# Conversion order of two networks' weights, and the turn of the global rows, in a fused attention and FFN kernel

## The chip, the cores and the metric

The kernel runs on one core of a Trainium2 chip. The metric is the device time of one execution in microseconds, from runs on the chip.

## The reference

Four batches of 8 heads attend locally (512 tokens, a window of 32 to each side, plus 32 global tokens); the 32 global rows of each batch attend to everything. The 2304 x 512 result goes through two feed-forward networks, the first gated, the second with a rational function in place of the gate:

```
x = attention(q_l, k_l, v_l, q_g, k_g, v_g)     # 2304 x 512
gate = 1 / (1 + exp(-(x @ w_gate)))
x = (gate * (x @ w_val)) @ w_out                # 512 -> 1536 -> 512
h = x @ w2_in                                   # 512 -> 2048
P = a0 + a1*h + a2*h*h + a3*h*h*h
Q = 1 + |b0|*|h| + |b1|*h*h
out = (P / (Q + 1e-6)) @ w2_out                 # 2048 -> 512
```

The inputs come as 64-bit numbers; the kernel turns their two 32-bit words into single precision itself.

## The kernel before

**Products.** Every product of the two networks is made of three matmuls on a high and a low part: line 710 to 712 for a first product (rows times inner weights), 828 to 830 for the second product of the gated network, 1240 to 1242 for that of the rational one. A weight therefore exists as a pair of halves, hi and lo.

**Conversion.** An item of weights comes as a raw DMA of 512 KB, and is then worked on by four engines: `magnitude` (two instructions on ScalarE, lines 564 and 565), `bits` (two on DVE, 572 and 573), `add` (one on POOL, 580), `hi` (a cast on ScalarE, 602) and `lo` (a subtraction on POOL, 610); most parts are then kept in DRAM and loaded again when they are wanted. For the gate and value weights `sums` (DVE, 627 to 630) and `splits` (ScalarE 639, POOL 640) make further combinations. `Weights.order` (from line 467) is the list of items: for each pair of slices of 128 columns (f, f+1) of the gated network the inner weights, its two output weights (w4out and w5out for f = 4 and so on), and in between some items of the rational network, `two`, as many as `AT_ONCE` says. `plan` turns the list into steps: item j is started while j-1 gets its bits and j-3 its hi and lo, so that the order of the list is the order in which weights become ready. In each pair of the gated network a `Pace` spreads the steps over 34 us, between the matmuls of that pair. Instructions stand on each engine in the order in which the program writes them.

**Gated network.** The rows are four tiles of 512 and one of 128, the global rows (tile index 4, `GLOB`). Tiles 0 and 1 and the global rows go pair by pair, p = 0 to 5, with first products, gate (sigmoid on ScalarE line 748, product on DVE 749, hi 756, lo 761) and second products of the pair before. Tiles 2 and 3 follow with a combined form of the first product (`strassen`). Second products are summed in `gacc` by DVE (line 842). A finished tile is *parked*: cast to hi on ScalarE (845) and subtracted to lo on DVE or POOL in turn (846), as the input yh, yl of the rational network.

**Rational network.** It works on 68 units: four groups of four slices of 128 columns, and in each group 17 units, four for each of four tiles and one for the global rows, all four slices at once. The tiles of a group follow `LAST_TURNS`. In step n of the loop (line 1273) the table `PLAN2` issues parts of units around n: `first(n)`, the rational function of the units n-1 and n-2 (last of it `quot`, DVE line 1190), `lo(n-3)` and `second(n-4)`; from unit 34 on the second product comes a step later. `first` stands behind `lo` in a step. For a unit of 512 rows `lo` is a subtraction on POOL (line 1211); for the global unit it is four transposes on TensorE (line 1206, out `rt`) of the result of `quot`, then a cast and a subtraction on DVE (1209), since its rows came turned. After each step the loop calls `rest(n)` (line 1107), which issues what is left of the gated network: the last two second products of tile 3 (`queue`), the parks of tiles 2 and 3 (`parks`) and `back(1)`, which loads the parked tile 1.

Of the kernel before, what the change touches and what calls it, by code (L numbers as in the profile page):

```python
# [29 lines left out]
LN_SCALE = 2.0**-32  # L30

TILES = [(0, 512), (512, 512), (1024, 512), (1536, 512), (2048, 128)]
GLOB, LAST_TURNS = 4, (0, 2, 4, 1, 3)


def tile_of(tok):
# [118 lines left out]
class Slots:  # L155


    def __init__(self, tiles):
        self.tiles, self.free, self.uses = tiles, list(tiles), {}
# [289 lines left out]
class Weights:  # L449
# [4 lines left out]


    EARLY, AHEAD = 4, 3
    AT_ONCE = (0, 2, 2, 1, 1, 4)
    RING2 = (4, 5, 6, 7, 0, 1, 2, 3, 8, 9, 10, 11)

    def __init__(self, tc, early, dram, ins, outs):  # L460
        self.nc, self.early, self.dram = tc.nc, early, dram
        self.late = self.only = None
        self.ins, self.outs = ins, outs
        self.have, self.staged, self.whole, self.kept = {}, {}, {}, {}
        NF = FF // 128
        inner = {f: [(1, f, "gv", h) for h in range(2)] for f in range(NF)}
        outer = {f: [(1, f, "out", 0)] for f in range(NF)}
        two = []
        for f in range(0, FF2 // 128, G2):
            two += [(2, f, "in", k) for k in range(4)] + [(2, f + g, "out", 0) for g in range(G2)]  # L470


        self.order = inner[0] + inner[1] + outer[0] + outer[1]
        ends, n = [len(self.order)], 0
        for p, f in enumerate(range(2, NF + 1, 2)):
            m = n + self.AT_ONCE[p]
            if f < NF:
                self.order += inner[f] + inner[f + 1] + two[n:m] + outer[f] + outer[f + 1]
            else:
                self.order += two[n:m]  # L480
            ends.append(len(self.order))
            n = m
        self.order += two[n:]
        ends.append(len(self.order))


        a, b = self.EARLY, self.EARLY + 1
        self.urgent = [(self.magnitude, a), (self.magnitude, b), (self.bits, a), (self.add, a), (self.bits, b), (self.add, b),
                       (self.hi, a), (self.lo, a), (self.hi, b), (self.lo, b)]
        self.plan = []  # L490
        for p in range(len(ends) - 1):
            out = []
            last = p == len(ends) - 2
            for j in range(ends[p], ends[p + 1] + (3 if last else 0)):
                for back, steps in ((3, (self.hi, self.lo)), (1, (self.bits, self.add)), (0, (self.magnitude,)),
                                    (4, (self.sums,)), (5, (self.splits,))):
                    i = j - back
                    if ends[0] <= i < len(self.order) and (back < 4 or self.order[i][0] == 1 and self.order[i][2:] == ("gv", 1)):
                        out += [(1.2 if back > 3 else 0.7, step, i) for step in steps]
            self.plan.append(out)  # L500


        self.loads = [(x,) for f in range(2) for x in inner[f]] + [(outer[f][0],) for f in range(2)]
        for f in range(2, NF):
            h = [(1, f, x, 0) for x in ("g0", "s2", "s1", "g1", "s3", "v1", "s4")]
            self.loads += [(h[0], h[1]), (h[2], h[3]), (h[4], h[5]), (h[6],)]
            if f % 2:
                self.loads += [(outer[f - 1][0],), (outer[f][0],)]
        self.loads += [(key,) for key in two]
        self.two = {key: self.RING2[n % 12] for n, key in enumerate(two)}  # L510
        self.loaded = self.limit = 0
        self.places, self.free = {}, [True] * 12
# [220 lines left out]
def gated(nc, pools, only, xpool, dram, wp, ident, xh, xl):  # L733
# [225 lines left out]
    def back(i):  # L959
        yh[i] = xpool.tile([128, 4, 512], F32R, tag=f"xh{i}", name=f"yh{i}")  # L960
        yl[i] = xpool.tile([128, 4, 512], F32R, tag=f"xl{i}", name=f"yl{i}")
        for m in range(4):
            t = wp.kept[9, i, "y", m]
            nc.sync.dma_start(yh[i][:, m].bitcast(F32), t[:, 0:512])
            nc.sync.dma_start(yl[i][:, m].bitcast(F32), t[:, 512:1024])
# [139 lines left out]
    pace.finish()  # L1105

    def rest(n):
        for _ in range({1: 2, 3: 2}.get(n, 0)):
            queue.pop(0)()
        for _ in range({2: 4, 4: 2, 5: 2}.get(n, 0)):  # L1110
            parks.pop(0)()
        if n == 5:
            back(1)

    return yh, yl, rest
# [276 lines left out]
```

## Time and profile before

| | |
|---|---|
| median of 3 runs | 923.63 us (923.0 to 925.52) |
| the profiled execution | 921.69 us |
| its span, first to last instruction | 919.9 us |
| granted clock of TensorE, mean | 0.996 |
| busy: TensorE, DVE, ScalarE, POOL | 98%, 81%, 63%, 63% |
| attention | 0 to about 115 us |
| gated pairs p = 0 to 5 | about 121 to 353 us |
| gated tiles 2 and 3 | about 348 to 527 us |
| rational network | 527.6 to about 905 us |

Engines are PE (TensorE), DVE (VectorE), ACT (ScalarE), POOL (GpSimd) and SP (the queue that issues DMAs). L748 is line 748 of the kernel. In a timeline row stand the start in us, the duration, engine, line and operation, out<-in, and in brackets how long the engine had been idle and what ended that. Rows of the same instruction overlap, since a matmul of 0.39 us is followed by the next after 0.23.

### The profile page before, as it was taken

Reading aid. Unit: us, or ns where it says so; the run is one execution under the profiler, and the core shown is the slowest. Engines: PE = TensorE matmul, PEld = TensorE weight load, DVE = VectorE, ACT = ScalarE, POOL = GpSimd, SP = SyncE. Lnnn points to the kernel's source line nnn. Section 1 sums busy time; section 2 is a strip of 40 time slices with the busy share of each in tenths; the row PEclk is TensorE's granted clock in tenths of the full one; section 3 lists DMA queues with packets and bytes.
Section 4 is the critical chain, followed back from the end, with each engine's and each line's share of the span. In section 5 each row is a group of like instructions: output and inputs, shape, how many; then the busy total and the mean of one; then the engine's idle time right before and its main releaser. Section 6 shows DMA issues by size and latency. Waiting matters only on the chain.

```text
span 919.9 us, 13698 instructions
## 1 busy us (share of the span) xinstructions
PE 897.2 (98%) x4666; PEld 743.5 (81%) x4666; DVE 747.0 (81%) x1297; ACT 579.1 (63%) x1161; POOL 576.0 (63%) x460
## 2 busy tenths in 40 slices
PE   8989999989999989999999998999999999999998
PEld 6778888878888868888888887888888888888886
DVE  6998866899988875867775769977788899988886
ACT  6988963555454434345444377777777787777773
POOL 5776763768667663567676766444456676666564
PEclk9999999999999999999999999999999999999999
DMA  9865263768667785689998943004000410020112
GB/s 306 241 207 171 82 245 122 245 238 286 250 222 260 242 282 218 234 297 338 344 340 303 374 177 109 1 1 153 30 1 1 141 43 0 3 91 1 46 57 92
DMA packets 60804, 156.23 MB, mean 170 GB/s; under 512 B 7104, under 2 KB 9152, under 8 KB 60736
## 3 DMA queue, kind: packets, MB, share of 16 engines
q1 hardware_dynamic: 60640, 155.24, 48.7%
q8 instruction: 37, 0.61, 0.3%
q14 instruction: 31, 0.25, 0.1%
q10 hardware_dynamic: 96, 0.13, 0.1%
HBM read 103.17 MB, written 52.17 MB: 169 GB/s over the span
## 4 chain that ended last, share of the span: by engine, by line
PE 71%; DVE 15%; issue 5%; ACT 5%; POOL 2%; DMA 1%; SPq 0%; POOLq 0%; ACTq 0%; DVEq 0%
PE rp L1240 7%; PE rp L1242 6%; PE rp L1241 6%; PE rp L712 6%; PE rp L711 6%; PE rp L710 6%; PE p L830 3%; PE p L828 3%; PE p L829 3%; DVE gacc L842 2%; PE pair L260 2%; PE pb L974 1%; PE pb L976 1%; PE pb L975 1%; PE bank L361 1%
## 5 line engine op out<-in xcount | busy, mean ns | idle before, releaser
L1157 POOL TENSOR_TENSOR v<-v,u 128x512 f32<-128x512 f32 x68 | 90.8, 1335 | 105.5 <-ACT v L1153 105.4
L1211 POOL TENSOR_TENSOR rgl<-t,rgh 128x512 fp32r<-128x512 f32 x64 | 90.7, 1417 | 41.0 <-POOL v L1157 17.9
L756 ACT CAST gh<-t 128x512 fp32r<-128x512 f32 x38 | 23.6, 620 | 92.2 <-DVE t L749 83.1
L1165 DVE TENSOR_TENSOR t<-rp,t 128x512 f32<-128x512 f32 x68 | 46.7, 687 | 41.5 <-ACT t L1161 40.3
L294 POOL TENSOR_TENSOR p<-p,r 128x448 f32<-128x448 f32 x64 | 58.9, 945 | 33.2 <-DVE r L289 20.2
L1150 ACT ACTIVATE u<-rp 128x512 f32<-128x512 f32 x68 | 40.5, 596 | 61.3 <-PE rp L712 58.2
L1190 DVE SCALAR_TENSOR_TENSOR t<-t,co,v 128x512 f32<-128x512 f32 x68 | 73.9, 1087 | 2.4
L1186 DVE SCALAR_TENSOR_TENSOR v<-v,u 128x512 f32<-128x512 f32 x68 | 74.7, 1098 | 0.0
L279 ACT ACTIVATE p<-p,mx 128x224 f32<-128x224 f32 x128 | 60.3, 481 | 6.5 <-DVE mx L271 6.5
L842 DVE TENSOR_TENSOR gacc<-p,gacc 128x512 f32<-128x512 f32 x80 | 51.5, 680 | 12.7 <-PE p L830 12.5
L1182 DVE SCALAR_TENSOR_TENSOR v<-v,u 128x512 f32<-128x512 f32 x68 | 58.3, 857 | 1.1 <-ACT u L1178 1.1
L761 DVE TENSOR_TENSOR gl<-t,gh 128x512 fp32r<-128x512 f32 x38 | 36.3, 955 | 27.8 <-ACT gh L756 27.8
L1153 ACT ACTIVATE v<-u,co 128x512 f32<-128x512 f32 x68 | 55.6, 817 | 2.3
L1174 ACT ACTIVATE u<-v,co 128x512 f32<-128x512 f32 x68 | 49.2, 723 | 6.1 <-POOL v L1157 6.0
L1161 ACT ACTIVATE t<-rp,co 128x512 f32<-128x512 f32 x68 | 51.8, 762 | 1.9 <-POOL rgl L1211 1.9
L1199 ACT CAST rgh<-t 128x512 fp32r<-128x512 f32 x64 | 39.1, 611 | 19.3 <-DVE t L1190 19.3
L1169 DVE SCALAR_TENSOR_TENSOR t<-t,co,rp 128x512 f32<-128x512 f32 x68 | 50.2, 738 | 0.0
L1178 ACT ACTIVATE u<-u,co 128x512 f32<-128x512 f32 x68 | 48.5, 713 | 2.3 <-DVE t L1165 2.2
L271 DVE CUSTOM_DVE_ANT_0 p<-pair,masks 128x224 f32<-128x224 f32 x128 | 42.2, 383 | 6.6 <-PE pair L260 5.5
L1265 POOL TENSOR_TENSOR racc<-ev,racc 128x512 f32<-128x512 f32 x22 | 37.9, 1742 | 0.0
L749 DVE TENSOR_TENSOR t<-pv,t 128x512 f32<-128x512 f32 x28 | 19.2, 684 | 19.5 <-PE pv L712 17.0
L260 PE MATMUL pair<-kn,qn 64*128 64x224 f32 x256 | 30.9, 374 | 1.0 <-DVE mx L271 0.4
(1344 smaller groups left out, 3177.7 us busy)
## 6 DMA issues: line engine op xcount, KB each, us to landing
raw1gv<-in_w_gate_val SPq DMA_DIRECT2D x24, 512.0 KB, 4.0
raw2in<-in_w_in SPq DMA_DIRECT2D x16, 512.0 KB, 5.6
raw2out<-in_w_out SPq DMA_DIRECT2D x16, 512.0 KB, 5.0
kn<-in_k_l SPq DMA_DIRECT2D x15, 448.0 KB, 5.9
raw1out<-in_w_out SPq DMA_DIRECT2D x12, 512.0 KB, 3.9
vn<-in_v_l SPq DMA_DIRECT2D x16, 256.0 KB, 4.3
out<-racc SPq DMA_DIRECT2D x16, 256.0 KB, 2.0
qn<-in_q_l SPq DMA_DIRECT2D x15, 256.0 KB, 4.7
```

The lines of the kernel that those rows point to most:

```text
L279: nc.scalar.activation(p, p, AF.Exp, bias=s["mx", half][:, n : n + 1], scale=-1.0, accum_out=s["sm", half][:, n, 0:1])
L294: nc.gpsimd.tensor_tensor(p, p, r, ALU.mult)
L710: nc.tensor.matmul(ps, wh, mh[:, k], start=k == 0, stop=False)
L711: nc.tensor.matmul(ps, wh, ml[:, k], start=False, stop=False)
L842: nc.vector.tensor_tensor(a, ps[m], a, ALU.add)
L1153: nc.scalar.activation(new(u, "v"), st[u]["u"], AF.Identity, bias=b0, scale=b1)
L1157: nc.gpsimd.tensor_tensor(s["v"], s["v"], s["u"], ALU.mult)
L1182: nc.vector.scalar_tensor_tensor(s["v"], s["v"], Q_CONST, s["u"], ALU.add, ALU.mult)
L1186: nc.vector.scalar_tensor_tensor(s["v"], s["v"], 2.0, s["u"], ALU.subtract, ALU.mult)
L1190: nc.vector.scalar_tensor_tensor(s["t1"], s["t1"], a0, s["v"], ALU.add, ALU.mult)
L1211: nc.gpsimd.tensor_tensor(s["gl"], s["t1"], s["gh"].bitcast(F32), ALU.subtract)
L1240: nc.tensor.matmul(ps, gh[:, w], wh, start=k == 0, stop=False)
```

## The change

Three edits. In `Weights.order` the two output weights of a pair now stand ahead of the rational items of that pair, and `AT_ONCE` moves one rational item from p = 1 to the last pair, p = 5. In `LAST_TURNS` the global rows take the second turn of each group of 17 units instead of the third, so that their unit is the fifth instead of the ninth. In `rest` the last two gated second products move from step 3 to step 2, behind first(2) and not behind first(3) as before, the parks of tile 2 from step 2 to step 3, and `back(1)` from step 5 to step 3.

```diff
--- before.py
+++ after.py
@@ -30,7 +30,7 @@
 LN_SCALE = 2.0**-32
 
 TILES = [(0, 512), (512, 512), (1024, 512), (1536, 512), (2048, 128)]
-GLOB, LAST_TURNS = 4, (0, 2, 4, 1, 3)
+GLOB, LAST_TURNS = 4, (0, 4, 2, 1, 3)
 
 
 def tile_of(tok):
@@ -454,7 +454,7 @@
 
 
     EARLY, AHEAD = 4, 3
-    AT_ONCE = (0, 2, 2, 1, 1, 4)
+    AT_ONCE = (0, 1, 2, 1, 1, 5)
     RING2 = (4, 5, 6, 7, 0, 1, 2, 3, 8, 9, 10, 11)
 
     def __init__(self, tc, early, dram, ins, outs):
@@ -475,7 +475,7 @@
         for p, f in enumerate(range(2, NF + 1, 2)):
             m = n + self.AT_ONCE[p]
             if f < NF:
-                self.order += inner[f] + inner[f + 1] + two[n:m] + outer[f] + outer[f + 1]
+                self.order += inner[f] + inner[f + 1] + outer[f] + outer[f + 1] + two[n:m]
             else:
                 self.order += two[n:m]
             ends.append(len(self.order))
@@ -1105,11 +1105,11 @@
     pace.finish()
 
     def rest(n):
-        for _ in range({1: 2, 3: 2}.get(n, 0)):
+        for _ in range({1: 2, 2: 2}.get(n, 0)):
             queue.pop(0)()
-        for _ in range({2: 4, 4: 2, 5: 2}.get(n, 0)):
+        for _ in range({3: 4, 4: 2, 5: 2}.get(n, 0)):
             parks.pop(0)()
-        if n == 5:
+        if n == 3:
             back(1)
 
     return yh, yl, rest
```

**ScalarE in the last gated pair, p = 5** (f = 10 and 11; t11_0 is the sigmoid of f = 11, tile 0; w111out0 the cast of the output weight of f = 11; st11s the splits). Before:

```order
L748 ACTIVATE t11_0_3720<-pg11_0_3694 128x512
L756 CAST gh11_0_3723<-t11_0_3720 128x512
L602 CAST w110out0_2_3727<-v110out0_3500 128x512
L748 ACTIVATE t10_glob_3764<-pgv10_3739 128x256
L564 ACTIVATE v23out0_3767<-raw2out30_3573 128x512
L565 ACTIVATE q23out0_3768<-raw2out30_3573 128x512
L748 ACTIVATE t10_1_3801<-pg10_1_3775 128x512
L756 CAST gh10_1_3804<-t10_1_3801 128x512
L639 CAST st11s2_3808<-v111gv0_3379 128x2x256
L639 CAST st11s4_3815<-v111gv1_3421 128x2x256
L602 CAST w111out0_4_3822<-v111out0_3576 128x512
```

And with the change:

```order
L748 ACTIVATE t10_0_3606<-pg10_0_3580 128x512
L756 CAST gh10_0_3609<-t10_0_3606 128x512
L602 CAST w110out0_0_3613<-v110out0_3456 128x512
L564 ACTIVATE v21out0_3649<-raw2out10_3483 128x512
L565 ACTIVATE q21out0_3650<-raw2out10_3483 128x512
L602 CAST w111out0_2_3675<-v111out0_3486 128x512
L748 ACTIVATE t11_0_3711<-pg11_0_3685 128x512
L756 CAST gh11_0_3714<-t11_0_3711 128x512
L564 ACTIVATE v22out0_3723<-raw2out20_3559 128x512
L565 ACTIVATE q22out0_3724<-raw2out20_3559 128x512
L639 CAST st11s2_3727<-v111gv0_3365 128x2x256
L639 CAST st11s4_3734<-v111gv1_3407 128x2x256
```

The cast of w111out moved from behind the splits and the sigmoid of tile 1 to a place ahead of the first sigmoid of f = 11.

**DVE at the start of the rational network** (t1.. and v.. are the rational function's values of the unit that the number names; gacc3 is tile 3's accumulation, yl2 the park of tile 2). Before:

```order
L1165 TENSOR_TENSOR t12_5774<-rp2_5757,t12_5774 128x512
L1182 SCALAR_TENSOR_TENSOR v1_5711<-v1_5711,u1_5709 128x512
L846 TENSOR_TENSOR yl2_5734<-gacc2_4171,yh2_5733 128x512 x2
L1169 SCALAR_TENSOR_TENSOR t12_5774<-t12_5774,co_79,rp2_5757 128x512
L1186 SCALAR_TENSOR_TENSOR v1_5711<-v1_5711,u1_5709 128x512
L1190 SCALAR_TENSOR_TENSOR t11_5713<-t11_5713,co_79,v1_5711 128x512
L1165 TENSOR_TENSOR t13_5813<-rp3_5796,t13_5813 128x512
L1182 SCALAR_TENSOR_TENSOR v2_5772<-v2_5772,u2_5770 128x512
L842 TENSOR_TENSOR gacc3_4325<-p210_3_0_5822,gacc3_4325 128x512
L842 TENSOR_TENSOR gacc3_4325<-p210_3_1_5823,gacc3_4325 128x512
L842 TENSOR_TENSOR gacc3_4325<-p210_3_2_5840,gacc3_4325 128x512
L842 TENSOR_TENSOR gacc3_4325<-p210_3_3_5841,gacc3_4325 128x512
```

And with the change:

```order
L1165 TENSOR_TENSOR t12_5774<-rp2_5757,t12_5774 128x512
L1182 SCALAR_TENSOR_TENSOR v1_5711<-v1_5711,u1_5709 128x512
L842 TENSOR_TENSOR gacc3_4325<-p210_3_0_5783,gacc3_4325 128x512
L842 TENSOR_TENSOR gacc3_4325<-p210_3_1_5784,gacc3_4325 128x512
L842 TENSOR_TENSOR gacc3_4325<-p210_3_2_5801,gacc3_4325 128x512
L842 TENSOR_TENSOR gacc3_4325<-p210_3_3_5802,gacc3_4325 128x512
L1169 SCALAR_TENSOR_TENSOR t12_5774<-t12_5774,co_79,rp2_5757 128x512
L1186 SCALAR_TENSOR_TENSOR v1_5711<-v1_5711,u1_5709 128x512
L1190 SCALAR_TENSOR_TENSOR t11_5713<-t11_5713,co_79,v1_5711 128x512
L1165 TENSOR_TENSOR t13_5843<-rp3_5826,t13_5843 128x512
L1182 SCALAR_TENSOR_TENSOR v2_5772<-v2_5772,u2_5770 128x512
L846 TENSOR_TENSOR yl2_5734<-gacc2_4171,yh2_5733 128x512 x2
```

The four additions to gacc3 moved ahead of the two yl2 subtractions, by one unit; the instructions themselves are the same.

**TensorE behind second(2)** (rp20_0_3 is the last bank of second(2), rp7 is first(7), rt the transposes of the global unit). Before, there, and at the place of the transposes four units later:

```order
L1240 MATMUL rp20_0_3_5896<-w22out0_62_5627,rgh2_5902 128x512
L1241 MATMUL rp20_0_3_5896<-w22out0_62_5627,rgh2_5902 128x512
L1242 MATMUL rp20_0_3_5896<-w22out0_62_5627,rgl2_5903 128x512
L710 MATMUL rp7_6016<-yh2_5733,w20in0_56_5379 128x512
L711 MATMUL rp7_6016<-yl2_5734,w20in0_56_5379 128x512
L712 MATMUL rp7_6016<-yh2_5733,w20in0_56_5379 128x512
```

```order
L1242 MATMUL rp20_2_3_6095<-w22out0_62_5627,rgl6_6102 128x512
L1206 MATMUL rt8_6189<-ident_66,t18_6081 128x128 x4
L710 MATMUL rp11_6202<-yh1_5958,w20in0_56_5379 128x512
L711 MATMUL rp11_6202<-yl1_5959,w20in0_56_5379 128x512
L712 MATMUL rp11_6202<-yh1_5958,w20in0_56_5379 128x512
```

And with the change:

```order
L1240 MATMUL rp20_0_3_5906<-w22out0_62_5627,rgh2_5912 128x512
L1241 MATMUL rp20_0_3_5906<-w22out0_62_5627,rgh2_5912 128x512
L1242 MATMUL rp20_0_3_5906<-w22out0_62_5627,rgl2_5913 128x512
L1206 MATMUL rt4_6008<-ident_66,t14_5892 128x128 x4
L710 MATMUL rp7_6021<-yh2_5733,w20in0_56_5379 128x512
L711 MATMUL rp7_6021<-yl2_5734,w20in0_56_5379 128x512
```

The transposes of the global unit moved from first(11) to first(7), and read the quotient t14 of unit 4 instead of t18 of unit 8.

## Rows read from the trace of the kernel before

**Rows 1.** The page's first part, TensorE: busy us, share, instructions.
```profile
PE 897.2 (98%) x4666; PEld 743.5 (81%) x4666; DVE 747.0 (81%) x1297; ACT 579.1 (63%) x1161; POOL 576.0 (63%) x460
```

**Rows 2.** TensorE's waits: waiting, releaser, us in total, times, longest us.
```profile
PE pv L710 <- ACT t L748: 2.8, 2, 2.4
PE rp L1240 <- DVE gacc L842: 2.8, 1, 2.8
PE p L830 <- POOL w111out L610: 2.8, 1, 2.8
PE p L828 <- ACT w111out L602: 1.7, 1, 1.7
```

**Rows 3.** TensorE's timeline around w111out.
```profile
331.38 0.39 PE L830 MATMUL p<-gh,w110out 128*128 128x512 f32 x1
...
340.94 0.40 PE L828 MATMUL p<-gh,w111out 128*128 128x512 f32 x1
```

**Rows 4.** Windows: length, busy PE PEld DVE ACT POOL, granted clock, DMA share, GB/s.
```profile
290.00:360.00 70.00, 65.54 (x294) 53.85 (x293) 55.08 (x68) 29.99 (x57) 45.34 (x32) 0.98 0.73 252
333.40:341.00 7.60, 4.78 (x13) 3.48 (x14) 6.87 (x6) 2.50 (x6) 5.72 (x5) 0.78 0.96 326
540.00:572.51 32.51, 29.74 (x125) 24.17 (x124) 30.74 (x38) 23.58 (x38) 20.23 (x14) 0.95 0.30 98
555.70:559.40 3.70, 3.68 (x10) 2.92 (x11) 3.66 (x6) 2.05 (x3) 1.79 (x2) 0.56 1.00 342
```

**Rows 5.** ScalarE's timeline, last gated pair.
```profile
319.39 0.60 ACT L748 ACTIVATE t<-pg 128x512 f32<-128x512 f32 x1 [1.19 <-PE pg L712]
...
332.81 0.61 ACT L602 CAST w111out<-v111out 128x512 fp32r<-128x512 f32 x1
```

**Rows 6.** POOL's timeline, last gated pair.
```profile
332.46 2.78 POOL L640 TENSOR_TENSOR st11s<-v111gv,st11s 128x512 fp32r<-128x512 f32 x2 [0.31 <-ACT st11s L639]
335.19 1.71 POOL L610 TENSOR_TENSOR w111out<-v111out,w111out 128x512 fp32r<-128x512 f32 x1
```

**Rows 7.** TensorE's timeline, pair of f = 4.
```profile
194.25 0.50 PE L710 MATMUL pv<-xh,w14gv 128*128 128x512 f32 x1 [2.40 <-ACT t L748]
```

**Rows 8.** ScalarE's timeline, pair of f = 4.
```profile
187.12 0.68 ACT L564 ACTIVATE v20in<-raw2in 128x512 f32<-128x512 f32 x1 [2.13 <-DMA raw2in<-in_w_in]
```

**Rows 9.** TensorE's timeline, rational network.
```profile
552.57 0.39 PE L1242 MATMUL rp<-w20out,rgl 128*128 128x512 f32 x1
555.72 0.79 PE L1240 MATMUL rp<-w20out,rgh 128*128 128x512 f32 x1 [2.77 <-DVE gacc L842]
...
559.39 0.39 PE L710 MATMUL rp<-yh,w20in 128*128 128x512 f32 x1
...
570.07 0.39 PE L1242 MATMUL rp<-w22out,rgl 128*128 128x512 f32 x1
570.30 0.39 PE L710 MATMUL rp<-yh,w20in 128*128 128x512 f32 x1
...
592.07 0.60 PE L1206 MATMUL rt<-ident,t 128*128 128x128 f32 x4
592.42 0.48 PE L710 MATMUL rp<-yh,w20in 128*128 128x512 f32 x1
```

**Rows 10.** DVE's timeline, rational network.
```profile
558.75 0.75 DVE L1190 SCALAR_TENSOR_TENSOR t<-t,co,v 128x512 f32<-128x512 f32 x1
...
567.74 1.36 DVE L846 TENSOR_TENSOR yl<-gacc,yh 128x512 fp32r<-128x512 f32 x1 [0.53 <-ACT yh L845]
...
570.84 1.67 DVE L1190 SCALAR_TENSOR_TENSOR t<-t,co,v 128x512 f32<-128x512 f32 x1
```

**Rows 11.** POOL's timeline, rational network: the first of three.
```profile
567.26 1.29 POOL L846 TENSOR_TENSOR yl<-gacc,yh 128x512 fp32r<-128x512 f32 x1 [1.80 <-DVE v L1182]
```

**Rows 12.** DVE's quot(38), and TensorE's first(41).
```profile
753.65 1.67 DVE L1190 SCALAR_TENSOR_TENSOR t<-t,co,v 128x512 f32<-128x512 f32 x1
...
753.50 0.39 PE L710 MATMUL rp<-yh,w28in 128*128 128x512 f32 x1
```

## The prediction

> **What bounds the kernel now.** I read four views. First the page's share of each engine: TensorE is busy for 98% of the span [rows 1], so only an idle TensorE, or one at the lower clock, can be won back. Then its list of waits [rows 2]: behind one wait of the attention on a DMA, which the change does not touch, stand exactly the three places that the three edits touch. These are 1.7 and 2.8 us on w111out, 2.8 us on the accumulation gacc, and 2.8 us in two pieces on the sigmoid of line 748. Then the timeline of TensorE and of its releaser around each place, and last the busy time and granted clock by stretch [rows 4], since a wait is not all that a stall costs. Over 333.4 to 341.0 the granted clock was 0.78 and over 555.7 to 559.4 it was 0.56: part of both stretches ran at 1.2 instead of 2.4 GHz, and before both TensorE had idled for 1.7 to 2.8 us. At the full clock one 512-column matmul follows the last after 0.23 us (570.07 to 570.30 [rows 9]; 0.227 over many). I count a stall as the time between two starts less 0.227 us for each matmul between.
>
> One execution was profiled; it took 921.69 us, of which the span is 919.9. The sum is made against 921.69. The median of the runs is 923.63, 1.94 above it, and I move the result by that.
>
> **Edit 1, last pair (A).** From 331.38 to 340.94 [rows 3] TensorE started 13 matmuls, 2.95 us at full clock, in 9.56: 6.6 us lost. The first part waited for the cast of w111out, which stood on ScalarE at 332.81 behind two splits [rows 5], the larger part for POOL's low half, which ran from 335.19 [rows 6] behind a 2.78 us split. Now the cast stands ahead of the sigmoid of f = 11, which ran at 319.39 [rows 5], some 12 us before TensorE wants the weight. The whole 6.6 goes: **-6.6**. Its bounds are 0 (it comes late again: a rival) and -6.6.
>
> **Edit 1, pair with f = 4 (C).** TensorE waited 2.40 us at 194.25 for the sigmoid [rows 7]. That sigmoid stood on ScalarE behind two rational weights, one of which waited 2.13 us for its DMA until 187.12 [rows 8], then behind v14out, a split that waited for DVE, and a cast. Now one gated weight takes that place, and what stood between goes behind the sigmoid. Its start would be 187.12 plus two instructions of 0.7, a cast of 0.6 and one of 0.4: 189.5, its end 190.1, against 191.85 where TensorE became idle (194.25 less 2.40). So **-2.4**, and the small second piece of the same wait, **-0.4**. Bounds: 0 and -2.8.
>
> **What edit 1 adds.** Four rational items become five in the last pair, and one of two goes from the second pair. No item is added in all. An item is two instructions on DVE, three on ScalarE, two on POOL. DVE was busy for 55.1 of 70 us between 290 and 360, ScalarE 30.0 and POOL 45.3 [rows 4], so 15 us of DVE hide it. The cover fails where an item's bit operations stand ahead of a gate product just when TensorE is done. The nearest rows are the waits of 0.4 and 2.4 us that such an item caused on ScalarE [rows 2]; I take **+0.8**, with 0 and +3 as ends. The DMAs of the moved items go with them; SP's rows at the seam stand in the same order. Later the conversions run the same items as before.
>
> **Edit 3 (B1).** At 555.72 second(0) of the rational part waited 2.77 us for the gated accumulation of tile 3 [rows 9], which stood on DVE behind two yl subtractions. The start at 559.39 came 6.82 us after 552.57, with 10 matmuls between: 4.55 lost, 1.6 of it at the lower clock (0.44 of 3.7 us [rows 4]). With the gated products in step 2, DVE adds gacc3 ahead of yl2 (second order fence), and this goes: **-4.6**. TensorE would come to the place where first(7) started, 570.30 [rows 9], at 565.7. The two parks of tile 2 that move behind it are wanted by first(5) only. That the call back(1) stands in an earlier step does nothing: SP issues the same rows, and its first load waits for a buffer that is released at the same place.
>
> **Edit 2 (B2).** Here the saving meets a new wait. The global unit becomes the fifth of 17, so its four transposes rt4 stand ahead of first(7) (third order fence), and they need quot(4), line 1190. DVE had to run the same 34 instructions from gacc2 to quot(4) in the old order and has to in the new one; only their order changes. Before they filled the stretch from 541 and ended at 570.84 + 1.67 = 572.51 [rows 10], with DVE busy for 30.7 of the 32.5 us up to there [rows 4]. So I take 572.5 for quot(4). TensorE, there at 565.7, idles some 6.8 us. The transposes take 0.4 (592.07 to the next matmul, 592.42, in the old place [rows 9]), so first(7) starts at 573.0 instead of 570.3: +2.7, which has B1's saving in it. I add 1.6 for the lower clock after the idle time, as after the two shorter ones, and take off 0.4 for the transposes that leave 592.07 [rows 9]. **B1 and B2 together: +3.9.** Below, DVE could be quicker if less of it met POOL: line 1190 took 1.67 against 0.75 alone [rows 10], three times 0.9, so 569.8 and +1.1 (without a loss of clock -0.5). Above, a longer stretch at the lower clock gives +6.
>
> Here a rule stands against the row. POOL's yl ran from 567.26 for 1.29 us [rows 11] while DVE's ran from 567.74 for 1.36 [rows 10]; if DVE had been shut out until 568.55, 0.55 us would be left for it, less than the 0.75 that an instruction of that size takes alone. So the two overlapped. The Trainium skill (SBUF — State Buffer, "Who interferes with whom") says that a DVE instruction with two SBUF inputs contends with a GpSimd one that reads SBUF, and that the shared pair is an exclusive lock. By that rule this unit's three POOL instructions and two of DVE would take 3 x 1.29 + 1.36 + 0.75 = 6.0 us one after the other, where 567.26 to 572.51 is 5.25; that estimate would make quot(4) 0.7 us later for each such unit.
>
> **Edit 2, later groups (B3).** The same transposes now stand ahead of first(24), first(41) and first(58). For the one in the slowest stretch, quot(38) ran 753.65 to 755.32 and first(41) started at 753.50 [rows 12], so TensorE would wait 1.8 us: **+1.9** with the transposes' own start. At the other two quot ended one to two us ahead, so nothing. Bounds 0 (DVE gains on TensorE in the 150 us before) and +3.5 (with a lower clock).
>
> **Sum.** -6.6 - 2.4 - 0.4 + 0.8 + 3.9 + 1.9 = -2.8. From 921.69 that is 918.9, and 920.8 against the median. A measurement of this kernel tells about 0.3% (2.8 us) from no change, so the likeliest case sits at the border of faster and the same. Its own range: -6.6 - 2.8 + 1.1 = -8.3, or 915.3, to -6.6 - 1 + 3 + 5 + 1.9 = +2.3, or 926.
>
> **Rivals.**
> 1. The transposes never wait (DVE is well ahead of its old time): then B1's 4.6 is kept. -6.6 - 2.8 - 4.6 + 0.8 = -13.2: 910.4. For it: DVE's order loses nothing, and gacc3 stands earlier. Against: the 34 instructions with DVE 95% busy. Chance 0.12.
> 2. Slower: the fifth item pushes DVE's gate products in the last pair back, TensorE waits there, and A returns in this form, with 3.9 and 1.9 still to pay. -2.8 + 0 + 3 + 3.9 + 1.9 = +6.0: 929.6; with half of A lost, 926.3. It decides from a wait of 3.5 us in all between 290 and 350. For it: the items stand in the most crowded stretch. Against: 15 us of idle DVE. Chance 0.17.
> 3. Edit 1 does not do what it says in pair f = 4 (the DMA of the gated weight is late there as the rational one was), and the rest as forecast: -2.8 + 2.8 = 0: 923.6. Chance 0.14.
> 4. Of two such instructions one shuts the other out, with two units of 0.7 each before quot(4) and 1.4 at quot(38): the sum grows by 2.8 to 0: 923.6. Chance 0.05, since the two instructions overlap [rows 10, 11].
>
> **How the numbers follow.** The forecast case has 0.52: 0.26 faster, 0.22 the same, 0.04 slower. Rival 1 is faster (0.12). Rival 2 is slower for 0.12 and the same for 0.05. Rivals 3 and 4: 0.04 faster, 0.12 the same, 0.03 slower. In all 0.42 faster, 0.39 the same, 0.19 slower. The predicted time is 920.8. The range from 913.5 to 926.5 leaves out most of rivals 1 and 2, about 0.2.
>
> **What would show it.** Right: no wait on w111out between 330 and 341; the sigmoid's wait near 194 gone; no wait on gacc at second(0); a wait of 4 to 7 us of TensorE on L1190 between 555 and 563 (all stands some 10 us earlier there), followed by matmuls of 0.63 us; one of 1 to 2 us at the third global unit. Wrong: no wait at L1206 (rival 1), or new waits on L749, L761 or L748 between 270 and 345 of over 3 us (rival 2).

## The result, and the profile after

The changed kernel took 929.03 us (median of 7 runs, 927.25 to 929.91) beside 923.94 for the kernel before: 1.0056 times its time, with a 95% interval of 1.0042 to 1.007. Forecast were 920.8 us and a range of 913.5 to 926.5, so it is slower by 0.6%, and outside the range. The profiled execution has a span of 926.8 us, 6.9 more than before.

TensorE's timeline, set against that of before at the same matmul, gives this ledger (us; minus is a gain):

| stretch | forecast | in the two traces |
|---|---|---|
| attention, which no edit touches | 0 | +0.5 |
| pair f = 4 (C) | -2.4 | -3.0 |
| pair f = 6, start and middle | -0.4 | +4.7 |
| w111out (A) | -6.6 | -6.6 |
| first pair of tile 2, near 365 | in +0.8 | +4.7 |
| one short stall near 386 that is gone | 0 | -0.3 |
| rational network to its second group (B) | +3.9 | +5.0 |
| unit 38 (B3) | +1.9 | +1.9 |
| sum | -2.8 | +6.9 |

TensorE's waits now read (columns as in [rows 2]; of its four lines the three on gacc and w111out are gone, and the one of pv on L748 now stands for another place):

```profile
PE rt L1206 <- DVE t L1190: 7.8, 2, 6.1
PE pg L710 <- ACT t L748: 3.8, 2, 2.8
...
PE pv L710 <- ACT t L748: 2.3, 1, 2.3
...
PE rp L1242 <- POOL rgl L1211: 0.7, 1, 0.7
```

Its timeline at the places of the ledger:

```profile
231.88 0.50 PE L710 MATMUL pv<-xh,w16gv 128*128 128x512 f32 x1 [2.33 <-ACT t L748]
...
252.56 0.50 PE L710 MATMUL pg<-xh,w16gv 128*128 128x512 f32 x1 [0.95 <-ACT t L748]
...
333.86 0.39 PE L828 MATMUL p<-gh,w111out 128*128 128x512 f32 x1
...
334.31 0.39 PE L830 MATMUL p<-gh,w111out 128*128 128x512 f32 x1
...
364.75 0.50 PE L710 MATMUL pg<-xh,w10gv 128*128 128x512 f32 x1 [2.82 <-ACT t L748]
...
573.33 1.11 PE L1206 MATMUL rt<-ident,t 128*128 128x128 f32 x4 [6.06 <-DVE t L1190]
...
760.33 0.66 PE L1206 MATMUL rt<-ident,t 128*128 128x128 f32 x4 [1.70 <-DVE t L1190]
```

The same matmuls in the kernel before, up to the first of tile 2:

```profile
232.46 0.50 PE L710 MATMUL pv<-xh,w16gv 128*128 128x512 f32 x1 [0.45 <-ACT t L748]
...
333.47 0.50 PE L828 MATMUL p<-gh,w111out 128*128 128x512 f32 x1 [1.70 <-ACT w111out L602]
...
336.96 0.67 PE L830 MATMUL p<-gh,w111out 128*128 128x512 f32 x1 [2.75 <-POOL w111out L610]
...
366.08 0.47 PE L710 MATMUL pg<-xh,w10gv 128*128 128x512 f32 x1
```

At 333.86 and 334.31 the brackets are gone: no wait on w111out. Where before there was one wait of 0.45 us on the sigmoid of f = 6, 2.33 us stand at 231.88 and 0.95 at 252.56. At 364.75 there is a wait that the kernel before did not have, and at 573.33 and 760.33 are the two at the transposes. What each stall cost beyond its wait is the clock after it (columns as in [rows 4]):

```profile
231.88:236.00 4.12, 4.12 (x11) 3.29 (x12) 3.44 (x6) 0.62 (x1) 3.84 (x4) 0.60 0.49 170
365.00:370.00 5.00, 5.00 (x16) 3.92 (x16) 4.32 (x7) 2.22 (x4) 1.28 (x1) 0.66 0.86 315
573.33:577.50 4.17, 4.17 (x12) 3.49 (x13) 3.51 (x6) 1.21 (x2) 0.00 (x0) 0.51 0.00 0
```

At a granted clock of 0.60, 0.66 and 0.51 the three stretches gave away 1.6, 1.7 and 2.0 us more.

Who was late can be followed on ScalarE:

```profile
227.62 0.68 ACT L564 ACTIVATE v20in<-raw2in 128x512 f32<-128x512 f32 x1 [1.93 <-DMA raw2in<-in_w_in]
...
229.40 1.14 ACT L639 CAST st6s<-v16gv 128x512 fp32r<-128x512 f32 x2 [0.55 <-DVE v16gv L629]
...
231.23 0.60 ACT L748 ACTIVATE t<-pg 128x512 f32<-128x512 f32 x1
...
251.39 0.62 ACT L602 CAST st20in<-v20in 128x512 fp32r<-128x512 f32 x1 [4.45 <-DMA k17s<-st7s]
...
351.29 0.62 ACT L845 CAST sty<-gacc 128x512 fp32r<-128x512 f32 x1 [3.29 <-DMA k90y<-sty]
...
354.56 0.66 ACT L564 ACTIVATE v24in<-raw2in 128x512 f32<-128x512 f32 x1 [2.65 <-POOL st22out L610]
...
355.69 0.57 ACT L748 ACTIVATE t<-pg 128x512 f32<-128x512 f32 x1
...
362.55 0.62 ACT L845 CAST sty<-gacc 128x512 fp32r<-128x512 f32 x1 [2.83 <-issue]
...
364.11 0.59 ACT L748 ACTIVATE t<-pg 128x512 f32<-128x512 f32 x1
```

The sigmoid of f = 6 (231.23) stands behind a rational weight that waited 1.93 us for its DMA and a split that waited for DVE; it starts 0.6 us earlier than in the kernel before (231.81), while TensorE comes 2.5 us earlier. At 251.39 a rational cast waited 4.45 us until the DMA that stores a split (k17s) gave back one of the three staging buffers, and the sigmoid stood right behind it. Near 365 the chain is longer. The park cast at 351.29 waited 3.29 us for a staging buffer; POOL's half of it, and behind that the low half of the rational weight w22out, came after it:

```profile
351.99 1.29 POOL L846 TENSOR_TENSOR sty<-gacc,sty 128x512 fp32r<-128x512 f32 x1 [3.06 <-ACT sty L845]
...
353.23 1.29 POOL L610 TENSOR_TENSOR st22out<-v22out,st22out 128x512 fp32r<-128x512 f32 x1
```

Only then was a value buffer free for the next weight (354.56, 2.65 us of wait), behind which stood a sigmoid (355.69), behind that DVE's gate product and its sums, behind those a park (362.55), and behind that the sigmoid at 364.11, for whose bank TensorE waited.

### The profile page after: what moved, and what is told of

Read it like the earlier page. It is cut to its first block, busy times and chain, and to the rows that moved or that the text cites. A ratio compares the mean times of both kernels' runs of the same rounds, so it can differ in the third digit from the quotient of the medians.

```text
span 926.8 us, 13699 instructions
## 1 busy us (share of the span) xinstructions
PE 900.2 (97%) x4666; PEld 745.8 (80%) x4666; DVE 740.7 (80%) x1297; ACT 578.8 (62%) x1161; POOL 572.2 (62%) x460
## 4 chain that ended last, share of the span: by engine, by line
PE 74%; DVE 12%; ACT 4%; issue 3%; POOL 3%; DMA 3%; SPq 1%; POOLq 0%; ACTq 0%; DVEq 0%
PE rp L710 6%; PE rp L712 6%; PE rp L711 6%; PE rp L1240 6%; PE rp L1242 6%; PE rp L1241 6%; PE p L830 3%; PE p L828 3%; PE p L829 3%; PE pair L260 2%; PE bank L379 2%; PE bank L361 2%; PE pb L974 1%; PE pb L976 1%; PE pb L975 1%
## 5 line engine op out<-in xcount | busy, mean ns | idle before, releaser
L1190 DVE SCALAR_TENSOR_TENSOR t<-t,co,v 128x512 f32<-128x512 f32 x68 | 70.1, 1031 | 2.4
L1161 ACT ACTIVATE t<-rp,co 128x512 f32<-128x512 f32 x68 | 51.8, 762 | 2.5 <-POOL rgl L1211 2.5
```

What stands on the lines that cost most here:

```text
L1190: nc.vector.scalar_tensor_tensor(s["t1"], s["t1"], a0, s["v"], ALU.add, ALU.mult)
```

## The experiments

"Front" below is the time from the first gated matmul to one fixed matmul of tile 2 (388.25 in the trace of before), "back" the rest of the span. The kernel before has 267.0 and 531.7 us, the changed one 266.5 and 538.6. Each is from one trace: where the code of a half is the same, fronts differ by up to 1.4 us and backs by up to 1.6.

**1. Edit 1 alone.**

```diff
-    AT_ONCE = (0, 2, 2, 1, 1, 4)
+    AT_ONCE = (0, 1, 2, 1, 1, 5)
...
-    self.order += inner[f] + inner[f + 1] + two[n:m] + outer[f] + outer[f + 1]
+    self.order += inner[f] + inner[f + 1] + outer[f] + outer[f + 1] + two[n:m]
```

> Edit 1 alone; the turns and the rest of the gated work stand as in the kernel before. Theory: what edit 1 wins it loses again further on, all ahead of the rational network: -2.6 at f = 4 and -6.6 at w111out, against +4.7 before and behind f = 6 and +4.4 at the first pair of tile 2 (TensorE waiting for the sigmoid near 365). Time about 923.5 (-0.5 to before), second(0) again waits 2.8 us on gacc, no wait on L1190. Rival: the waits near 232 and 365 come from something else (the profile of one execution), then 9 us of gain stay and the time is about 915.

921.84 us, 0.9987 of before (0.9973 to 1.0): near the theory's 923.5, far from 915. The waits at 232 (2.35 us), 253 (1.01) and 365 (2.65) are there again, front 265.7, back 531.7. So most of the gain of edit 1 is lost within the gated network. Against the expectation the transposes of the third turn waited 0.95 us on L1190; so they did in experiments 2 and 3 (1.0 us each), where as here TensorE had lost less at second(0) than in the kernel before (last section).

**2. The order alone, the items as before.**

```diff
     AT_ONCE = (0, 2, 2, 1, 1, 4)
...
-    self.order += inner[f] + inner[f + 1] + two[n:m] + outer[f] + outer[f + 1]
+    self.order += inner[f] + inner[f + 1] + outer[f] + outer[f + 1] + two[n:m]
```

> Only the order in edit 1: output weights ahead of the rational items, but the numbers of items per pair as before (two, two, one, one, four). Theory: the fifth item in the last pair is what makes the sigmoid near 365 late (its staging buffer and its steps run into the parks), so that wait is gone, w111out still comes early (-6.6), and the time is about 917 to 919. Rival: the order alone pushes the rational items into the parks; then 2 to 4.5 us of wait on L748 near 365 stay, and the time is 920 to 924.

917.73 us, 0.9948 (0.9929 to 0.9968). w111out is in time and the wait near 365 is gone; what is left on the sigmoid is at f = 4 and in the middle of pair f = 6:

```profile
PE pv L710 <- ACT t L748: 2.7, 1, 2.7
PE pg L710 <- ACT t L748: 1.5, 1, 1.5
```

So the fifth item causes the late sigmoid near 365, not the order. But the park cast waited for its staging buffer here as well, nearly as long as in the changed kernel (3.29 us):

```profile
349.65 0.62 ACT L845 CAST sty<-gacc 128x512 fp32r<-128x512 f32 x1 [2.93 <-DMA k90y<-sty]
350.18 0.67 ACT L564 ACTIVATE v24in<-raw2in 128x512 f32<-128x512 f32 x1
```

```profile
344.54 1.75 POOL L610 TENSOR_TENSOR st22out<-v22out,st22out 128x512 fp32r<-128x512 f32 x1
```

What differs more is POOL's order. The low half of w22out stands at 344.54, ahead of that park, and the next weight starts at once (350.18); with the fifth item it stands behind the park (353.23), and the next weight starts 4.4 us later (354.56), 2.65 us of it waiting for POOL.

**3. The items alone, in the old order.**

```diff
-    AT_ONCE = (0, 2, 2, 1, 1, 4)
+    AT_ONCE = (0, 1, 2, 1, 1, 5)
```

> Only the numbers of items in edit 1 (none, one, two, one, one, five), with the old order inside a pair. Theory: the wait at f = 4 goes by the item that leaves its pair, not by the order, and the wait near 365 comes by the fifth item; w111out stays late in the old order (1.7 and 2.8 us with slow matmuls): -2.6 to -4 at 194, lost again at 232 to 253 where the pair still has two items, plus 2.7 or more at 365: 924 to 927. Rival: order and items act together; then the sigmoid at f = 4 still waits 2 us or more.

922.35 us, 0.9993 (0.9975 to 1.0011). The theory's causes held at both ends: the wait at f = 4 is gone without the order, so it was the item (2.31 us come back at 232), and the one near 365 is there, though shorter than the 2.7 us expected. But w111out did not wait as long as in the old order before:

```profile
334.05 0.50 PE L830 MATMUL p<-gh,w111out 128*128 128x512 f32 x1 [1.54 <-POOL w111out L610]
...
363.54 0.50 PE L710 MATMUL pg<-xh,w10gv 128*128 128x512 f32 x1 [1.69 <-ACT t L748]
```

One wait of 1.54 us stands where two of 1.7 and 2.8 were expected: the moved item shifted the casts here too, which was not foreseen, and the time came below the 924 to 927 expected.

**4. The items spread over later pairs, in the new order.**

```diff
-    AT_ONCE = (0, 2, 2, 1, 1, 4)
+    AT_ONCE = (0, 1, 1, 2, 2, 4)
```

(with the order of experiment 2)

> Only edit 1's order, with the ten rational items spread as none, one, one, two, two and four over the pairs instead of none, two, two, one, one, four. Theory: the waits on L748 near 194 (2.7 us and 1.5 of slow clock after it in the run with the order alone) and near 253 (1.5) come from the two items each that two early pairs carry on a DVE and a staging ring without room, and the later pairs have that room: both waits gone, 4 to 5 us below the run with the order alone, about 913. Rival: room is short in every pair, so the waits come back on L748 or L749 near 270 to 310; then 917 to 920.

918.16 us, 0.9952 (0.9933 to 0.9971): the rival's time. The waits at 194, 232 and 253 are gone, and the same pair of waits stands one pair further on, at f = 8:

```profile
271.33 0.50 PE L710 MATMUL pv<-xh,w18gv 128*128 128x512 f32 x1 [2.14 <-ACT t L748]
...
291.82 0.50 PE L710 MATMUL pg<-xh,w18gv 128*128 128x512 f32 x1 [0.71 <-ACT t L748]
```

The next pair, with two items as well, shows none; but TensorE came late to f = 10 here, after the two waits, and experiments 11 and 12 show one there. So two rational items in one of these pairs make its successor's sigmoid late, and TensorE waits there where it comes early enough.

**5. Edits 2 and 3 without edit 1.**

```diff
-GLOB, LAST_TURNS = 4, (0, 2, 4, 1, 3)
+GLOB, LAST_TURNS = 4, (0, 4, 2, 1, 3)
...
-        for _ in range({1: 2, 3: 2}.get(n, 0)):
+        for _ in range({1: 2, 2: 2}.get(n, 0)):
...
-        for _ in range({2: 4, 4: 2, 5: 2}.get(n, 0)):
+        for _ in range({3: 4, 4: 2, 5: 2}.get(n, 0)):
...
-        if n == 5:
+        if n == 3:
```

> Edits 2 and 3 without edit 1. Theory: the quotient of unit 4 ends when DVE has run its 34 instructions, so TensorE waits about 6 us at L1206 and then runs some 4 us at the lower clock: +5.0 for the first group and +1.9 at unit 38, about 930.8. Rival: the wait was made longer by TensorE's earlier arrival through edit 1; then under 4 us of wait and about 927.

931.53 us, 1.0089 (1.0063 to 1.0115); the transposes waited 6.12 us, back 538.3, which is 6.6 more than before for the 6.9 of the theory. As it said: edits 2 and 3 are what makes the kernel slower.

**6. Edit 2 alone.**

```diff
-GLOB, LAST_TURNS = 4, (0, 2, 4, 1, 3)
+GLOB, LAST_TURNS = 4, (0, 4, 2, 1, 3)
```

> Edit 2 alone: the global rows as the second turn, the gated products and parks in the steps of the kernel before. Theory: quot(4) ends when DVE has done its work, near 572.5 on the clock of the kernel before, whether edit 3 is there or not; so second(0) waits 2.8 us on gacc as before, the transposes then 1.5 to 2.5 instead of 6.1, and unit 38 1.7 us: 926 to 928, some 3 us below edits 2 and 3 together, because one stall takes the place of two and the clock falls less. Rival: edit 3 is worth its 4.4 us here too, then this is 4 us slower than both together, 935.

929.76 us, 1.0062 (1.004 to 1.0083). The wait came as expected, 2.0 us:

```profile
575.60 0.66 PE L1206 MATMUL rt<-ident,t 128*128 128x128 f32 x4 [2.01 <-DVE t L1190]
```

```profile
573.90 1.64 DVE L1190 SCALAR_TENSOR_TENSOR t<-t,co,v 128x512 f32<-128x512 f32 x1
```

The time missed the 926 to 928 expected. Back is 537.6, 0.7 less than with edit 3, which is within what backs of the same code differ by: the stall at second(0) with its slow matmuls and the one of 2 us, with slow matmuls too, cost nearly what the one of 6 us costs. Set against the trace of before by the shift ahead of the rational network (3.1 us), quot(4) ends at 572.4; in the changed kernel, with no shift, at 573.3. So with the global rows as the second turn edit 3 moves TensorE's wait, and no gain of it can be told.

**7. Edit 3 alone.**

```diff
-        for _ in range({1: 2, 3: 2}.get(n, 0)):
+        for _ in range({1: 2, 2: 2}.get(n, 0)):
```

> Edit 3 alone, with the old turns: the last gated second products in step 2, ahead of tile 2's parks in the same step; the global rows stay the third turn. Theory: the wait of second(0) on gacc goes with the slow matmuls behind it, and nothing takes its place since the transposes stand at 592 as before: -4.4, about 919.5. Rival: the parks of tile 2, now behind four more additions on DVE, make first(4) wait 2 to 4 us; then 921 to 924.

922.13 us, 1.0 (0.9987 to 1.0013): the time is the rival's, but its mechanism did not show, and the theory's gain did not stay. second(0) no longer waits and first(4) waits for nothing, but of the 4.3 us that TensorE won there against the kernel before, it lost 3.5 again between 571 and 593:

```profile
PE rp L1240 <- DVE racc L1259: 1.5, 1, 1.5
...
PE rt L1206 <- DVE t L1190: 1.0, 1, 1.0
...
PE rp L1242 <- POOL rgl L1211: 0.3, 1, 0.3
```

DVE was busy for 43.7 of the 45.0 us around it (fourth figure):

```profile
547.00:592.00 45.00, 43.01 (x186) 34.31 (x184) 43.66 (x51) 36.19 (x58) 29.77 (x20) 1.00 0.21 71
```

**8. The whole change, transposes behind first(u+3).**

```diff
+        turn = None
...
+            if name == "lo" and 0 <= u < len(units) and units[u][1] == GLOB:
+                turn = u
+                continue
+            if name == "abs" and turn is not None:
+                lo(turn)
```

> The whole change, with the transposes of a global unit issued behind first(u+3) and not ahead of it. Theory: the quotient comes when DVE has done its instructions, whatever TensorE does, so the 6.1 us of wait at the transposes shrink by first's twelve matmuls, 2.7 us, to 3.4, the 1.7 us at unit 38 go: about 4.5 below the changed kernel, 924 to 925. Rival: the wait is one of the pipeline (each unit waits for the one before it), and moves along with first: 6 us stay, 929.

924.34 us, 1.0014 (1.0001 to 1.0027), as the theory said. The wait is 3.43 us, 2.6 less for 2.7 us of matmuls put ahead of it, and the one at unit 38 is gone:

```profile
574.27 1.12 PE L1206 MATMUL rt<-ident,t 128*128 128x128 f32 x4 [3.43 <-DVE t L1190]
```

quot(4) ended at 574.2, or 573.4 less the 0.9 us by which all stands later there: the same moment as in the changed kernel. So it did not depend on when TensorE came.

**9. The whole change, the parks' low halves on POOL.**

```diff
-                    (nc.vector if m % 2 else nc.gpsimd).tensor_tensor(
+                    (nc.vector if m % 2 and i < 2 else nc.gpsimd).tensor_tensor(
```

> The whole change, with all low halves of the parks of tiles 2 and 3 on POOL (four subtractions of 1.4 us taken from DVE). Theory: DVE's work ahead of quot(4) is what TensorE waits for at the first transposes; without 5.5 us of it the wait of 6.1 falls to 1 to 2 us, and with it most of the slow matmuls: 923 to 925. Rival: POOL is then what is late (its parks ahead of rgl and of the product of line 1157), and TensorE waits as long, on yl or on rgl: 927 or more.

928.35 us, 1.0059 (1.0042 to 1.0077): the rival. POOL was held by the parks, and DVE, relieved, sat idle for 6.9 us in three waits for ScalarE's line 1161, two of which (6.4 us) lead back to POOL's rgl; the longest of POOL's rows and of DVE's waits:

```profile
554.75 5.89 POOL L846 TENSOR_TENSOR yl<-gacc,yh 128x512 fp32r<-128x512 f32 x4 [0.98 <-ACT yh L845]
```

```profile
562.74 0.69 DVE L1165 TENSOR_TENSOR t<-rp,t 128x512 f32<-128x512 f32 x1 [4.45 <-ACT t L1161]
```

quot(4) came no earlier (575.1, or 573.8 less 1.3 of shift), and TensorE waited 1.5 us on yl and 1.5 on rgl as well. So POOL has no room for this work: DVE's list sets quot(4), and POOL's lies right behind it. ScalarE, busy for 22.6 of the 32.3 us in the changed kernel, was not tried.

**10. The order alone, edit 3, global rows as the fourth turn.**

```diff
-GLOB, LAST_TURNS = 4, (0, 2, 4, 1, 3)
+GLOB, LAST_TURNS = 4, (0, 2, 1, 4, 3)
```

(with the order of experiment 2 and the line of experiment 7)

> Edit 1's order alone plus edit 3's place for the gated products, with the global rows as the fourth turn (their transposes eight units later than in the changed kernel). Theory: DVE is the bound from 540 to about 592, and catches up with TensorE by some 0.8 us per unit once the parks are done; so the 4.4 us that TensorE wins at second(0) are lost where it first waits for DVE within eight units, in smaller pieces (racc, rgl or L1190): time 916 to 918, no more than 1 us below the run with the order alone. Rival: the early transposes alone took the gain; then 913 to 914.

917.04 us, 0.9935 (0.9909 to 0.996), as the theory said: 1.5 us on racc and 0.7 on rgl take back part of the gain, and no transposes wait. Beside experiment 2 it is 0.7 us, which the two intervals do not tell apart.

**11. The best version: one item in each of the first four pairs.**

```diff
-GLOB, LAST_TURNS = 4, (0, 2, 4, 1, 3)
+GLOB, LAST_TURNS = 4, (0, 2, 1, 4, 3)
...
-    AT_ONCE = (0, 2, 2, 1, 1, 4)
+    AT_ONCE = (1, 1, 1, 1, 2, 4)
```

(with the order of experiment 2 and the line of experiment 7)

> A version that may beat both: edit 1's order with the items spread as one, one, one, one, two and four, edit 3's place for the gated products, and the global rows as the fourth turn. Theory: a pair with one rational item costs no wait, so the ones near 194, 232, 253, 271 and 292 all go, and the later pair with two did not wait in the run with the items spread: w111out -6.6, all else before the rational network -3.3, and 2 of 4.4 us at second(0): 911 to 914. Rival: the first pair has no room for an item (it had none before): a wait of 2 us or more on L748 near 155 to 165, and 915 to 918.

912.09 us, 0.9873 (0.9855 to 0.9892), faster than both kernels. The first pair had room for its item; one wait of 0.7 us on a sigmoid is left:

```profile
PE rp L1240 <- DVE racc L1259: 1.5, 1, 1.5
...
PE pv L710 <- ACT t L748: 0.7, 1, 0.7
```

```profile
305.47 0.50 PE L710 MATMUL pv<-xh,w110gv 128*128 128x512 f32 x1 [0.69 <-ACT t L748]
```

It stands at the start of f = 10, behind the only early pair that still carries two items. Front 257.6, back 530.0.

**12. The same without its edits of the rational network.**

```diff
-    AT_ONCE = (0, 2, 2, 1, 1, 4)
+    AT_ONCE = (1, 1, 1, 1, 2, 4)
```

(with the order of experiment 2)

> The best version without its two edits of the rational network: edit 1's order with one, one, one, one, two and four items, the old turns and the old place of the gated products. Theory: where a pair carries one item its sigmoid is not late, so the conversions give the whole of it before the rational network (some 8 us), but second(0) waits 2.8 us on gacc with slow matmuls, and the transposes near 584 wait another 1 to 1.5 us: 914 to 916, 2 to 3 us above the best version. Rival: the two edits of the rational network carry as much as the items; then 918 or more, as in the run with the order alone.

913.85 us, 0.9892 (0.9871 to 0.9912), 0.15 below the 914 expected at least. second(0) waited 2.8 us, as expected; the transposes did not; at f = 10 the sigmoid was late again (0.80 us). Front 257.8, back 531.9: nearly the whole gain is in the conversions. The two edits of the rational network give some 2 us by these numbers, though the two intervals overlap.

## Why the prediction was wrong

The forecast of -2.8 and the +6.9 in the traces lie 9.7 us apart. Of these, 5.1 stand in pair f = 6 and 3.9 near 365, so the steps that failed are the ones on edit 1's conversions; the rational network has 1.1.

**A was right and stayed right:** -6.6 forecast, -6.6 measured; the order does it, and experiment 2 keeps most of it to the end (4.8 us, by its ratio).

**C failed as a gain, in the step "So -2.4, and the small second piece of the same wait, -0.4".** The wait at 194 went (-3.0 for the pair). But that second piece at 232 was read as a stall to be removed, and was the sign that the conversions of the next pair had no room: they kept their time to 0.6 us while TensorE came 2.5 earlier, and a wait of 2.3 us with 1.6 of slow clock took its place, then one of 1 us at a staging buffer. Experiments 3, 4, 11 and 12 show the cause: the wait stands each time behind a pair with two rational items. The forecast moved TensorE and left its suppliers' order in place without asking when they would be done.

**"What edit 1 adds" was mis-sized and its place was missed:** +0.8 (0 to +3) forecast, +4.7 measured near 365. The step "so 15 us of DVE hide it" counted DVE's idle time over 70 us; what was late was a chain through three staging buffers and the orders of POOL and ScalarE behind them. Experiment 2, without the fifth item, has no such wait of TensorE, though its park cast waited 2.93 us for a buffer; there the low half of w22out stood ahead of the park on POOL. Rival 2 named the fifth item as the mechanism, with the wrong engine and a place that ended 15 to 20 us too early, and a chance of 0.17. It gave 929.6 and the measurement 929.03, but its sum kept C and lost A, so the agreement of the totals is chance.

**B had the right mechanism, with a term put at nothing.** quot(4) was forecast for 572.5 and ended at 573.3; TensorE waited 6.06 us and not 6.8, since second(2) had waited 0.7 on rgl ahead of it and TensorE came later; the slow clock took 2.0 and not 1.6. Together +5.0 for +3.9. What was left out is that B1 has no worth of its own: experiment 7 shows 3.5 of its 4.3 us lost again within 40 us even without edit 2. As the forecast took quot(4) from DVE's list, the sum did not suffer from that. That list bears out well: counted from the first matmul of the rational network, quot(4) ends after 44.9 to 45.1 us in all seven traces with the old `rest`, under either turn and after whatever waits of TensorE. It ends after 44.2 in the three in which only the gated products moved (experiments 7, 10 and 11), and after 45.7 in the three in which tile 2's parks and back(1) moved as well (the changed kernel, experiments 5 and 8). So moving the parks, which the prediction put at nothing since they are wanted late, goes with 1.5 us of quot(4); no run moved them alone, nor back(1). B3 was exact.

**The rule that was weighed** was set against rows that do not speak against it. DVE's 34 instructions up to quot(4) took 32.3 us in the changed kernel and 31.6 before, but DVE was busy for 29.8 us of it in both (fourth figure; the first row is of before):

```profile
540.96:572.51 31.55, 28.78 (x120) 23.37 (x120) 29.78 (x37) 22.76 (x37) 19.89 (x13) 0.95 0.31 101
```

```profile
540.97:573.28 32.31, 25.56 (x110) 20.04 (x108) 29.75 (x37) 22.62 (x37) 19.93 (x13) 0.96 0.30 98
```

The 0.8 us between them are longer waits for ScalarE (0.47 on L1161, and 0.86 in place of 0.53 ahead of the first yl). So DVE met no more of POOL than before, and rival 4 did not occur. But "So the two overlapped", on which its chance rested, does not follow. A row can hold time in which its instruction waits, as the ends show. In the trace of before the two engines took turns there. POOL's three instructions end at 568.55 [rows 11], 570.25 and 571.96:

```profile
568.51 1.74 POOL L1211 TENSOR_TENSOR rgl<-t,rgh 128x512 fp32r<-128x512 f32 x1
570.21 1.75 POOL L1157 TENSOR_TENSOR v<-v,u 128x512 f32<-128x512 f32 x1
```

```profile
569.68 1.12 DVE L1186 SCALAR_TENSOR_TENSOR v<-v,u 128x512 f32<-128x512 f32 x1
```

DVE's yl, this one and quot(4) end at 569.10, 570.80 and 572.51 [rows 10], each 0.55 us behind one of POOL's. The same holds over the whole trace for lines 846, 878, 1182, 1186 and 1190, which read two operands from SBUF: in 105 of 105 cases that started with over 0.25 us of a POOL instruction to go, DVE ended 0.54 to 0.55 us behind POOL, and took 0.86 to 1.83 us; of the other 113 all but two took 0.67 to 0.76, and those two began 0.01 and 0.03 us ahead of a POOL instruction and ended 0.55 us behind it as well. Lines 842, 1165 and 1169, which read one operand from PSUM, took 0.67 to 0.75 with or without POOL. The Trainium skill (SBUF — State Buffer, "Who interferes with whom") calls the port pair that the two engines share an exclusive lock. The trace agrees, by these 0.55 us. The prediction's 6.0 us for this unit added up whole rows, and DVE's 1.36 has some of its wait in it; the 5.25 us measured are already the time with turns taken, so there was nothing to add.

**How the parts stand to the whole.** Edit 1 alone gave about -1 us, edits 2 and 3 alone some +8 (+6 to +11 by the interval, from four runs), and all three +5.1; single profiled executions differ by up to 3 us in when the gated network begins (121.3 to 124.3) with the same code ahead of it, so the ledger's half microseconds are not to be taken as exact. The range was narrower than its own terms: with the ends that the prediction gives to C (0), to edit 1's additions (+3), to B (+6) and to B3 (+3.5), and A kept, the sum is +5.9 and the time 929.5; the range took -1, +3, +5 and +1.9.

## What to carry to other kernels

A small wait at a place is a reading of that supplier's slack: zero. Before a stall upstream is counted as won, go to the next place where the same supplier was just in time, move the bound engine forward by the gain, and see whether the supplier can follow; if its own list is full, the gain is gone there. Where work is moved within a list, look at the buffers it borrows (here three staging buffers shared by three kinds of work) and at who stands behind it on each engine that works on it, not at the idle share of any engine. And of what was changed together here, one part (the order, 0.9948) was worth having, and the parts beside it cost more than it gave.

## What was not expected of the hardware

A stall of about the same length did not always lower TensorE's clock. In the changed kernel the wait of 2.82 us at 364.75 was followed by 0.66 of granted clock over 5 us (above). In experiment 1 a wait of 2.65 us by the same instruction was followed by none:

```profile
365.00:370.00 5.00, 4.98 (x22) 4.13 (x23) 4.31 (x6) 2.12 (x4) 1.28 (x1) 1.00 0.87 301
```

while in experiment 6 a wait of only 2.01 us was followed by 0.65:

```profile
575.60:580.00 4.40, 4.40 (x15) 3.60 (x16) 3.85 (x6) 1.21 (x2) 0.00 (x0) 0.65 0.00 0
```

The plainest case is second(0), where one instruction waited 2.75 to 2.77 us on gacc in seven traces. Over the 3.7 us behind it the granted clock was 0.56 in the kernel before [rows 4], 0.50, 0.65 and 0.58 in experiments 4, 6 and 12, and 1.00 in experiments 1, 2 and 3; in experiment 1:

```profile
555.31:559.01 3.70, 3.70 (x16) 3.10 (x17) 3.66 (x6) 2.04 (x3) 1.78 (x2) 1.00 0.88 332
```

So 1.6 to 2.0 us may come on top of such a wait or not, and the length of the wait alone did not tell which. The 1.6 that the prediction put into B1 is from the one execution that was profiled, and the same trace has a wait of 2.40 us, at 194.25 [rows 7], that was followed by 1.00 over 4 us.
